# ScalarE's cast of an activation's upper part, issued behind the output copy instead of ahead of it

## The chip, the cores and the metric

The kernel runs on one core of a Trainium2 chip. Its time is the device time in microseconds (us) of one execution; a median over several runs is compared, and less is better. The engines are TensorE (PE; its weight loads are shown as PEld), VectorE (DVE), ScalarE (ACT), GpSimd (POOL) and SyncE (SP, which here only issues DMAs).

## The reference

Agent attention, and behind it a gated feed-forward network over all its outputs:

```python
B, N, C = (4, 12480, 128); n_agents = 49; d_ff = 2048
def sm(a, b):                                  # softmax over the last axis
    s = scale * (a @ b.transpose(0, 2, 1))
    e = np.exp(s - s.max(-1, keepdims=True))
    return e / (e.sum(-1, keepdims=True) + 1e-09)
agent_v = sm(agents, k) @ v
x = (sm(q, agents) @ agent_v).reshape(B * N, C)
h = x @ w_in
out = (h * (1.0 / (1.0 + np.exp(-1.702 * h)))) @ w_out
```

## The kernel before, in words

The work is cut into 52 blocks of 960 tokens (13 for each of the four batches), two halves of 480 columns each. Since agent_v @ w_in is made once per batch (the weights wh and wl), a block's way is: scores of its queries against the 49 agents, softmax, transposed probabilities (q_hi, q_lo), and then 16 slices of 128 of the 2048 hidden columns. The next batch's keys and values are worked off in between, in the first three batches.

Precision is held by splitting 32-bit numbers into an upper and a lower part. Per slice f:

- `up` (L460 on): three pairs of matmuls into two banks `ph`, one for each half of the tokens, and two gelus on ACT (L480), which write `g`.
- `high` (L486 on): `gh`, the upper part of `g`. For even slices, and for 1 and 9, a DMA that POOL issues casts it (L489); for the six others (3, 5, 7, 11, 13, 15) ACT casts it (L491).
- `low` (L494 on): DVE subtracts, `gl` = g - gh (L496).
- `down` (L499 on): three pairs of matmuls, twice per slice, which add the slice's part to the block's output in the two banks `po0` and `po1`.

Most of PE's matmuls use half of its rows, and two run side by side (`half_matmul`, L192); a pair is meant by that. The `po` banks exist once (`ps_o` has one buffer of each), so the next block's first down product can start only when `store` (L522 on) has copied the last block's output out: ACT copies `po0` (L526), DVE copies `po1` (L528), and SP stores both.

No scheduler orders PE, ACT, DVE and POOL: the order in which the code writes their instructions is the order in which they are issued (`manual_schedule`, L847). It is written out gap by gap: `gap(t)` issues first the jobs of that gap (scores, softmax, keys, values), then the up product of a slice with its gelus (`do_up`), the subtraction of the slice three before it (`do_low`), and the down products of the slice six before it (`do_downs`). A block has 17 gaps, k = 0 to 16; in gap 1 there is no up product. In gap 16 `do_downs` holds the block's last down product and then `store`; the slice whose up product and gelus stand in that gap is slice 5 of the next block, one of those that ACT casts. In gap 0 of the next block come its follower's query scores, the up product of slice 6, and the first down product into the `po` banks. A cast by DMA is not issued in its own gap, but at the end of the next one (the list `late`); ACT's cast is written straight behind the gelus:

```python
        if by_dma(f):
            late.append(u)
        else:
            do_high(u)
```

The functions that the change touches, with the line numbers of the profile:

Of the kernel before, what the change touches and what calls it, by code (L numbers as in the profile page):

```python
# [40 lines left out]
def kernel(  # L41
# [140 lines left out]
    def rest():  # L182

        n, ins = order
        if ins is not None and (not rests or rests[-1][0] < n):
            rests.append([n, ins, None])
# [273 lines left out]
    def up(f, wts, pairs):  # L460
        wh, wl = wts
        q_hi, q_lo = pairs
        cols = slice(f * P, (f + 1) * P)
        ph = [ps_h.tile([P, 512], F32, name="ph") for _ in range(2)]
        products = [(wh, q_hi), (wh, q_lo), (wl, q_hi)]
        for k, (w, q) in enumerate(products):
            for c in range(2):
                r = slice(c * H, c * H + A)
                half_matmul(
                    ph[c].name,  # L470
                    c,
                    out=ph[c][:, :CH],
                    lhsT=w[r, cols],
                    rhs=q[r],
                    start=(k == 0),
                    stop=(k == 2),
                )
        g = gpool.tile([P, 2, CH], F32, name="g", bufs=G_BUFS)
        for c in range(2):
            nc.scalar.activation(out=g[:, c, :], in_=ph[c][:, :CH], func=AF.Gelu_apprx_sigmoid)  # L480
        return g

    def by_dma(f):
        return f % 2 == 0 or f in BY_DMA

    def high(f, g):  # L486
        gh = gpool.tile([P, 2, CH], F32R, name="gh", bufs=GH_BUFS)
        if by_dma(f):
            nc.gpsimd.dma_start(out=gh, in_=g)  # L489
        else:  # L490
            nc.scalar.copy(out=gh, in_=g)  # L491
        return gh
# [285 lines left out]
    po = {}  # L778

    late = []  # L780

    def do_high(u):
        gh[u] = high(u % NF, g[u])

    def do_up(u):
        n, f = divmod(u, NF)
        g[u] = up(f, wts[n // NG], pairs[n])
        if by_dma(f):
            late.append(u)
        else:  # L790
            do_high(u)
        if f == NF - 1:
            pairs.pop(n)

    def do_low(u):
        if 0 <= u < steps:
            gl[u] = low(g.pop(u), gh[u])
# [11 lines left out]
    def gap(t):  # L809
        n, k = divmod(t - LAG, GAPS)  # L810
        final = n == B * NG - 1
        if t < LAG:
            u = t
        elif final:
            u = n * NF + LAG + k
        elif k == 1:
            u = None
        else:
            u = n * NF + LAG + max(k - 1, 0)
        before, late[:] = list(late), []  # L820
        rest()
        for job in at.pop(t, ()):
            job()
        if u is not None:
            if u < steps:
                do_up(u)
                rest()
            do_low(u - 3)
        if t >= LAG:
            do_downs(n, k)  # L830
        for u in before:
            do_high(u)

    def do_downs(n, k):
        if k == 0:
            po[n] = [ps_o.tile([P, 512], F32, name=f"po{c}") for c in range(2)]
        first_whole = NF - LAG - 1 if n == B * NG - 1 else NF
        if 0 < k <= first_whole:
            do_down(n, k - 1, True)
        if k < first_whole:  # L840
            do_down(n, k, False)
        elif k < NF:
            do_down_whole(n, k)
        else:
            store(*divmod(n, NG), po.pop(n))

    with tc.manual_schedule(engines={E.PE, E.Activation, E.DVE, E.Pool}):  # L847
        for t in range(gaps):
            gap(t)
# [39 lines left out]
```

## Time and profile before

| | us |
|---|---|
| median of 3 runs (2022.54 to 2028.25) | 2024.57 |
| the profiled execution | 2026.61 |
| its span, first to last instruction | 2024.8 |
| PE busy (share of the span) | 1953.1 (96%) |
| DVE busy | 1553.4 (77%) |
| ACT busy | 1404.0 (69%) |
| POOL busy | 303.4 (15%) |

The profiled execution is one of its own, 2.04 us above the median. Busy time is the union of an engine's instructions. The ends of matmuls are modelled, and a pair's records overlap those of the next, so PE's idle time is a rough figure, and the starts of its matmuls are the sharper one. In a timeline each row gives start and duration in us, engine, line, operation, what it writes and reads, the shape, how many instructions were merged, and in brackets the engine's idle time ahead of it with what ended it.

### The profile page before, as it was taken

What the parts mean: (1) busy time and instruction counts of PE and PEld (TensorE: products, weight loads), DVE (VectorE), ACT (ScalarE), POOL (GpSimd) and SP (SyncE); (2) the same over time, 40 slices, a digit from 0 to 9 for tenths busy, and PEclk for the clock granted to TensorE, in tenths of its full rate; (3) what the DMA queues carried; (4) which work ended last, traced back from release to release, by engine and by line L of the source; (5) the groups of instructions that cost most, each with busy time, mean ns of one, the idle gap of its engine ahead of it and who ended that gap; (6) DMA issues with size and microseconds to landing.
All of it is one profiled execution on the core that took longest, in us unless ns stands there. A gap on an engine that the chain in (4) does not pass through costs nothing.

```text
span 2024.8 us, 59521 instructions
## 1 busy us (share of the span) xinstructions
PE 1953.1 (96%) x25158; PEld 1771.6 (87%) x25158; DVE 1553.4 (77%) x2025; ACT 1404.0 (69%) x2407; POOL 303.4 (15%) x642
## 2 busy tenths in 40 slices
PE   8789999999999999999999999999999999999998
PEld 8578998988988989998988889888898998999987
DVE  5687878887878888887867887888886766676765
ACT  3267777767667667677667677777776787777775
POOL 3011111111111111111111111111111111111111
PEclk9689999999999999999999999999999999999999
DMA  9555565666545665656554566566654544545453
GB/s 256 153 166 178 195 186 183 192 192 195 175 160 191 194 191 184 196 181 182 186 167 167 190 203 190 183 186 186 186 172 139 176 170 172 174 171 180 167 177 137
DMA packets 124336, 365.98 MB, mean 181 GB/s; under 512 B 12572, under 2 KB 38492, under 8 KB 124068
## 3 DMA queue, kind: packets, MB, share of 16 engines
q0 software_dynamic: 74880, 255.62, 36.6%
q1 hardware_dynamic: 49188, 106.55, 19.5%
q8 instruction: 197, 3.23, 0.7%
q14 instruction: 71, 0.58, 0.1%
HBM read 80.97 MB, written 25.56 MB: 53 GB/s over the span
## 4 chain that ended last, share of the span: by engine, by line
PE 80%; ACT 8%; DVE 4%; issue 4%; DMA 3%; SPq 0%; POOL 0%; ACTq 0%; DVEq 0%; POOLq 0%
PE po L192 46%; PE ph L192 24%; PE ps_m L192 7%; ACT g L480 3%; DMA gh<-g 2%; ACT L480 1%; DVE gl L496 1%; ACT L406 1%; PE ph L261 1%; ACT o L526 1%; PE ps_m L383 1%; ACT score L321 1%; DVE rest L173 0%; PE po L657 0%; PE po L518 0%
## 5 line engine op out<-in xcount | busy, mean ns | idle before, releaser
L480 ACT ACTIVATE g<-ph 128x480 f32<-128x480 f32 x1664 | 850.8, 570 | 474.3 <-PE ph L192 469.4
L496 DVE TENSOR_TENSOR gl<-g,gh 128x960 fp32r<-128x960 f32 x832 | 944.5, 1152 | 239.8 <-DMA gh<-g 177.8
L192 PE MATMUL po<-gh,wo_h 64*128 64x480 f32 x3300 | 799.0, 383 | 23.1 <-ACT o L526 18.1
L192 PE MATMUL po<-gl,wo_h 64*128 64x480 f32 x3300 | 789.0, 378 | 0.0
L192 PE MATMUL po<-gh,wo_l 64*128 64x480 f32 x3300 | 787.3, 377 | 0.0
L489 POOL DMA_DIRECT2D gh<-g x520 | 275.2, 529 | 1677.6 <-PE ph L192 799.5
L192 PEld LDWEIGHTS po<-gh,wo_h 64*128 64x128 f32 x3300 | 460.2, 185 | 62.7 <-ACT o L526 36.7
L192 PEld LDWEIGHTS po<-gh,wo_l 64*128 64x128 f32 x3300 | 461.9, 185 | 19.7
L192 PEld LDWEIGHTS po<-gl,wo_h 64*128 64x128 f32 x3300 | 463.2, 186 | 17.0
L192 PE MATMUL ph<-q_hi,wh 49*128 49x480 f32 x1664 | 431.8, 406 | 9.1 <-ACT g L480 8.3
L192 PE MATMUL ph<-q_lo,wh 49*128 49x480 f32 x1664 | 405.6, 380 | 0.0
L192 PE MATMUL ph<-q_hi,wl 49*128 49x480 f32 x1664 | 402.1, 379 | 0.0
L491 ACT CAST gh<-g 128x960 fp32r<-128x960 f32 x312 | 311.5, 998 | 9.9
L192 PEld LDWEIGHTS ph<-q_hi,wh 49*128 49x128 f32 x1664 | 237.5, 186 | 44.6 <-ACT g L480 29.1
L192 PEld LDWEIGHTS ph<-q_hi,wl 49*128 49x128 f32 x1664 | 237.6, 186 | 9.9 <-DVE wl L387 0.2
L192 PEld LDWEIGHTS ph<-q_lo,wh 49*128 49x128 f32 x1664 | 237.3, 188 | 6.1
L192 PE MATMUL ps_m<-ag_part,rest 64*128 64x49 bf16 x4320 | 143.2, 182 | 9.4 <-DVE rest L173 8.3
L192 PEld LDWEIGHTS <-rest 64*128 64x128 bf16 x4320 | 121.9, 94 | 11.9 <-DVE rest L173 11.3
L173 DVE TENSOR_TENSOR rest<-rest 128x488 bf16<-128x488 f32 (+1 forms) x182 | 131.0, 720 | 0.0
L192 PE MATMUL ps_m<-ag_part,qt 64*128 64x49 bf16 x2448 | 85.5, 184 | 0.2 <-DVE acc L354 0.2
L192 PEld LDWEIGHTS <-qt 64*128 64x128 bf16 x2448 | 68.7, 94 | 18.4 <-issue 14.2
L192 PEld LDWEIGHTS <-kt 64*128 64x128 bf16 x1872 | 50.2, 94 | 20.7 <-issue 20.1
(102 smaller groups left out, 1279.7 us busy)
## 6 DMA issues: line engine op xcount, KB each, us to landing
gh<-g POOLq DMA_DIRECT2D x520, 480.0 KB, 3.2
kt<-kT SPq DMA_DIRECT2D x52, 480.0 KB, 4.1
qt<-qT SPq DMA_DIRECT2D x52, 480.0 KB, 4.6
vt<-v SPq DMA_DIRECT2D x52, 480.0 KB, 5.3
outT<-o SPq DMA_DIRECT2D x104, 240.0 KB, 2.4
words<-w_in SPq DMA_DIRECT2D x4, 512.0 KB, 5.9
words<-w_out SPq DMA_DIRECT2D x4, 512.0 KB, 6.4
ag_sb<-agT SPq DMA_DIRECT2D x1, 98.0 KB, 2.0
```

The lines of the kernel that those rows point to most:

```text
L173: nc.vector.tensor_sub(out=halves(r)[1][:, s], in0=r[:, s], in1=halves(r)[0][:, s])
L192: ins = nc.tensor.matmul(tile_position=(c * H, 0), **kw)
L261: nc.tensor.matmul(out=ps[:TB, j * 2 * A : (j + 1) * 2 * A], lhsT=kt[:, c * KB // 2 + j, :], rhs=ag_sb[:, 0:2, :].rearrange("p b a -> p (b ...
L321: nc.scalar.activation(out=sc, in_=sc, func=AF.Exp, scale=scale)
L383: nc.tensor.matmul(out=pw[:, i], lhsT=w["avT"], rhs=w_in_sb[:, s], start=True, stop=True)
L406: nc.scalar.activation(out=e, in_=e, func=AF.Exp, scale=scale)
L480: nc.scalar.activation(out=g[:, c, :], in_=ph[c][:, :CH], func=AF.Gelu_apprx_sigmoid)
L489: nc.gpsimd.dma_start(out=gh, in_=g)
L491: nc.scalar.copy(out=gh, in_=g)
L496: nc.vector.tensor_sub(out=gl, in0=g, in1=gh.bitcast(F32))
L526: nc.scalar.copy(out=o, in_=po[c][:, :CH])
```

## The change

ACT's cast of a slice is no longer issued in `do_up`. The slice is put on a list, `soon`, and its cast is issued at the end of the same gap, behind the down products and, in a block's last gap, behind the output copies; it comes behind the casts by DMA of that gap.

```diff
     late = []
+    soon = []
 ...
         g[u] = up(f, wts[n // NG], pairs[n])
-        if by_dma(f):
-            late.append(u)
-        else:
-            do_high(u)
+        (late if by_dma(f) else soon).append(u)
 ...
         if t >= LAG:
             do_downs(n, k)
-        for u in before:
+        for u in before + soon:
             do_high(u)
+        soon.clear()
```

What this moves: the order of PE's, DVE's and SP's instructions, and what they wait for, is the same in both programs. On ACT, the order differs only around the output copy, once per block. This is ACT at the end of a late block and at the start of the next; `g<-ph` are gelus, two for each slice, `gh<-g` is the cast of one, `o<-po` the copy of the output. Before:

```order
L480 ACTIVATE g<-ph 128x480 x8
L491 CAST gh<-g 128x960
L480 ACTIVATE g<-ph 128x480 x4
L491 CAST gh<-g 128x960
L526 COPY o<-po_34851 128x480
L480 ACTIVATE g<-ph 128x480 x4
L491 CAST gh<-g 128x960
L480 ACTIVATE g<-ph 128x480 x2
L406 ACT_TABLE_LOAD
```

The same place in the changed program:

```order
L480 ACTIVATE g<-ph 128x480 x8
L491 CAST gh<-g 128x960
L480 ACTIVATE g<-ph 128x480 x4
L526 COPY o<-po_34851 128x480
L491 CAST gh<-g 128x960
L480 ACTIVATE g<-ph 128x480 x4
L491 CAST gh<-g 128x960
L480 ACTIVATE g<-ph 128x480 x2
L406 ACT_TABLE_LOAD
```

The copy and the cast of slice 5 have changed places; the other casts, here the one ahead and the one behind, stand where they stood, since no other work of ACT lies between the two places in their gaps. All 51 boundaries between blocks read alike; beside the copy at the run's very end no cast stands.

On POOL, the order is the same, but the tiles `gh` are drawn from their seven buffers in another order, so a casting DMA may wait for other earlier users of its buffer. These are the casts by DMA of slices 1, 2, 4, 6 and 8 around a late boundary, with the semaphores that each waits for. Before:

```order
L489 DMA gh_34113<-g_34064 128x960 [waits PE_49,DMASW5_49,DVE_49,Activation_49]
L489 DMA gh_34144<-g_34095 128x960 [waits PE_49,DVE_49,DMASW6_49,Activation_49]
L489 DMA gh_34202<-g_34155 128x960 [waits PE_49,DVE_49,DMASW7_49,Activation_49]
L489 DMA gh_34336<-g_34261 128x960 [waits PE_49,DVE_49,Activation_49]
L489 DMA gh_34424<-g_34379 128x960 [waits PE_49,DMASW1_49,DVE_49,Activation_49]
```

And in the changed program:

```order
L489 DMA gh_34113<-g_34064 128x960 [waits PE_49,DMASW1_49,DMASW5_49,DVE_49,Activation_49]
L489 DMA gh_34142<-g_34095 128x960 [waits PE_49,DMASW2_49,DVE_49,Activation_49]
L489 DMA gh_34200<-g_34155 128x960 [waits PE_49,DMASW3_49,DVE_49,Activation_49]
L489 DMA gh_34336<-g_34261 128x960 [waits PE_49,DVE_49,Activation_49]
L489 DMA gh_34424<-g_34379 128x960 [waits PE_49,DMASW1_49,DVE_49,Activation_49]
```

[...]

## Rows read from the trace of the kernel before

**Rows 1.** The page, part 1: busy us of each engine, share, instructions

```profile
PE 1953.1 (96%) x25158; PEld 1771.6 (87%) x25158; DVE 1553.4 (77%) x2025; ACT 1404.0 (69%) x2407; POOL 303.4 (15%) x642
```

**Rows 2.** Waits of PE: who waited for whom, us in total, times, longest

```profile
PE po L192 <- ACT o L526: 18.1, 46, 1.1
...
PE po L192 <- DVE o L528: 2.2, 4, 1.3
```

**Rows 3.** Timeline of ACT around one boundary of two blocks

```profile
1820.19 1.03 ACT L480 ACTIVATE g<-ph 128x480 f32<-128x480 f32 x2 [0.94 <-PE ph L192]
1821.26 1.00 ACT L491 CAST gh<-g 128x960 fp32r<-128x960 f32 x1
1822.16 0.55 ACT L526 COPY o<-po 128x480 f32<-128x480 f32 x1
...
1826.40 1.03 ACT L480 ACTIVATE g<-ph 128x480 f32<-128x480 f32 x2 [2.76 <-PE ph L192]
```

**Rows 4.** Timeline of PE at the same boundary

```profile
1821.91 0.45 PE L192 MATMUL ph<-q_hi,wl 49*128 49x480 f32 x2
1822.76 0.49 PE L192 MATMUL po<-gh,wo_h 64*128 64x480 f32 x2 [0.40 <-ACT o L526]
1823.09 0.38 PE L192 MATMUL po<-gl,wo_h 64*128 64x480 f32 x2
...
1823.53 0.25 PE L192 MATMUL ps_m<-ag_part,qt 64*128 64x49 bf16 x6
...
1824.15 0.47 PE L192 MATMUL po<-gh,wo_h 64*128 64x480 f32 x2
```

**Rows 5.** Timeline of DVE at the same boundary

```profile
1821.08 0.67 DVE L528 COPY o<-po 128x480 f32<-128x480 f32 x1
...
1825.44 2.22 DVE L496 TENSOR_TENSOR gl<-g,gh 128x960 fp32r<-128x960 f32 x2
```

**Rows 6.** Timeline of PE inside a block, undisturbed

```profile
1850.40 0.58 PE L192 MATMUL po<-gl,wo_h 64*128 64x480 f32 x2
...
1851.27 0.57 PE L192 MATMUL po<-gh,wo_l 64*128 64x480 f32 x2
```

**Rows 7.** Timeline of PE and DVE at a boundary with DVE's copy later

```profile
715.68 0.64 DVE L528 COPY o<-po 128x480 f32<-128x480 f32 x1
715.77 0.40 PE L192 MATMUL ph<-q_hi,wl 49*128 49x480 f32 x2
...
717.88 0.47 PE L192 MATMUL po<-gh,wo_h 64*128 64x480 f32 x2
```

**Rows 8.** Timeline of PE and DVE at a boundary without a wait for ACT

```profile
1054.92 0.65 DVE L528 COPY o<-po 128x480 f32<-128x480 f32 x1
...
1055.02 0.40 PE L192 MATMUL ph<-q_hi,wl 49*128 49x480 f32 x2
...
1056.93 0.47 PE L192 MATMUL po<-gh,wo_h 64*128 64x480 f32 x1
```

**Rows 9.** Timeline of PE and DVE at a boundary with DVE's copy latest

```profile
1245.42 1.16 DVE L496 TENSOR_TENSOR gl<-g,gh 128x960 fp32r<-128x960 f32 x1 [0.77 <-DMA gh<-g]
...
1245.72 0.39 PE L192 MATMUL ph<-q_hi,wl 49*128 49x480 f32 x2
...
1246.49 0.65 DVE L528 COPY o<-po 128x480 f32<-128x480 f32 x1
...
1247.20 0.48 PE L192 MATMUL po<-gh,wo_h 64*128 64x480 f32 x1 [0.28 <-DVE o L528]
...
1248.51 0.47 PE L192 MATMUL po<-gh,wo_h 64*128 64x480 f32 x1
```

**Rows 10.** Timeline of PE at two other boundaries, the second the run's last

```profile
1283.15 0.49 PE L192 MATMUL po<-gh,wo_h 64*128 64x480 f32 x2 [0.59 <-ACT o L526]
...
1993.42 0.49 PE L192 MATMUL po<-gh,wo_h 64*128 64x480 f32 x2 [1.10 <-ACT o L526]
```

**Rows 11.** The page, part 5: POOL's casting DMAs, busy, mean ns, idle before

```profile
L489 POOL DMA_DIRECT2D gh<-g x520 | 275.2, 529 | 1677.6 <-PE ph L192 799.5
```

## The prediction

> **What bounds the kernel now.** I read the busy shares first: TensorE (PE) is busy for 96% of the span, and ScalarE (ACT), the engine that the change reorders, for 69% [rows 1]. So ACT's order counts only where PE waits for ACT. The waits of PE come next: of all that PE waited for, the largest is ACT's copy of the output, 18.1 us in 46 waits, none over 1.1 us [rows 2]. There are 51 boundaries between two blocks, so this wait stands at 46 of 51, about 0.4 us each.
>
> One boundary shows why. ACT ends the two gelus of the slice at 1821.22, casts until 1822.26, and copies the output only then, 1822.16 to 1822.71 [rows 3]. PE is done with that block's last product long before; it has gone on to the next block's scores and its up product, whose last pair starts at 1821.91, and then needs the bank that ACT has not emptied: the first down product starts at 1822.76, 0.05 us after the copy ended [rows 4]. VectorE (DVE) copies the other half and was done at 1821.75 [rows 5]. So ACT's copy is the last of the two here, and it is late because a cast of about 1 us, which PE needs much later, stands ahead of it.
>
> **What the wait really costs.** The profile's idle time at this boundary is 0.40 us, counted from the end that it gives to the last up matmul. I count from start to start. Undisturbed pairs of 480 columns start every 0.215 us (1850.40 to 1851.27 holds four steps, 0.87 us) [rows 6]. From the first start of the last up pair to the scores behind the first down product there are four such steps, so 0.86 us; it took 1821.91 to 1823.53, 1.62 us [rows 4]. That is 0.76 us lost by the pair's first matmul; its second started 0.07 us later (1821.98), which leaves 0.69 us. I take 0.69, since the later half must be through too. The difference from 0.40 has two parts: a follow-on pair would have started before the modelled end of the one ahead, and the first step after the wait is 0.33 us (1822.76 to 1823.09) instead of 0.215 [rows 4].
>
> [...] By the idle times alone the sum would be the second rival's.
>
> **The change, part by part.** Nothing is added or taken away; PE, DVE and SyncE keep their order. On ACT only one thing per block moves: at the boundary, the copy goes ahead of the cast. At the other five casts of a block no ACT work lies between the old place and the new one, so these cost nothing.
>
> The copy. It can start where the cast stood, 1821.26, and end at 1821.81, about 0.9 us earlier; PE could take the bank 0.05 us later, 1821.86, ahead of the undisturbed start at 1821.91 + 0.215 = 1822.13. DVE's 1821.75 is ahead too. So the wait goes entirely, with 0.27 us to spare. The copy also waits for the down product ahead of it; DVE's copy, which waits for the same product, started at 1821.08, ahead of the gelus' end at 1821.22 [rows 3, 5], so ACT will not stand there. [...]
>
> The cast. It ends where the copy ended before, 0.45 us later than now. Its reader, DVE's subtraction for that slice, is the second of the two that start at 1825.44, so it starts at 1826.50, 3.8 us behind 1822.71 [rows 5]: covered. Past that cover each us would cost 1 us per block.
>
> What is late next in the block? The gelus behind the cast start as now. ACT then stands idle for 2.76 us until the following up product [rows 3], so PE's 0.69 us comes out of that idle time and is not given back; about 2.07 us of it stays.
>
> The buffers of the upper part. They are now taken in another order, so the DMA issues on GpSimd (POOL) wait for other earlier users. These issues mostly wait for PE (799.5 us before their kind) [rows 11], and PE's wait is unchanged in kind; I take 0. What could come of it reaches PE only through DVE's copy, for which PE waited 2.2 us in 4 waits [rows 2], so the bounds are -2.2 and +2.2 us.
>
> The boundaries, read one by one in the timeline, are of five kinds:
> - 29 like the one above, with DVE's copy done in time. At 25 the loss is 0.69 us: 17.3 us. At four PE stands longer; one of them has 0.59 us of idle time where [rows 4] has 0.40 [rows 10], 0.19 us more, so 0.69 + 0.19 = 0.88 us each: 3.5 us.
> - 10 at which DVE's copy ends 0.4 to 0.7 us after the last up pair's start, so DVE takes over. One: from last up pair to second down product 715.77 to 717.88, 2.11 us, DVE's copy ending at 716.32 [rows 7]. A boundary at which ACT was in time and DVE alone was late like that took 1055.02 to 1056.93, 1.91 us [rows 8]. The gain there is 0.20 us; at those where DVE is later it is near none. I take 0.14 on average: 1.4 us.
> - 6 at which DVE's copy is 1 us and more late, as at 1246: PE gets its second half only at 1247.20, released by DVE [rows 9]. Gain 0.
> - 5 without a wait for ACT, such as [rows 8]. Gain 0.
> - The last one, where no scores lie between and PE waits 1.10 us [rows 10]. The copy comes 0.9 us earlier: 0.9 us.
>
> Sum: 17.3 + 3.5 + 1.4 + 0 + 0 + 0.9 = 23.1 us.
>
> **The rivals.**
> First, DVE becomes the later of the two at the 29 good boundaries too. Against it: there its copy mostly ends some 0.2 us ahead of the last up pair's start, and PE's gain shifts both alike. If it happened, each would gain 2.24 - 1.91 = 0.33 us (1821.91 to 1824.15, the second down product [rows 4], against [rows 8]): 9.6 + 1.4 + 0.9 = 11.9 us.
>
> Second, only the idle time of the profile comes back, because the slow restart and the distance to the modelled end have another cause. The idle times at the 29 boundaries add up to 12.2 us, the ten would give 1.1 and the last 0.9: 14.2 us.
>
> Third, slower: the copy, stored 0.9 us earlier, and the loads behind it on SyncE's queue meet the DMAs that cast the even slices, and DVE's subtraction ahead of its copy waits for its cast. [rows 9] has this: 0.77 us of waiting for the DMA, copy done at 1247.14, and PE's second half at 1247.20. There the second down product came 2.79 us after the last up pair (1245.72 to 1248.51), against 2.24 at 1822. If all 29 went so: 29 x 0.55 = 16.0 us slower. It decides from DVE's copy being 0.96 us later than now (1822.71, where ACT's copy ends today, against 1821.75); below that there is a gain. Against it: at 1821 the subtraction ahead of DVE's copy was done by 1821.08, when the copy began [rows 5], before that block's store can be issued, with the change too.
>
> Fourth, the change does nothing that counts: PE waited for something else that becomes ready at the same time. Against it stands the 0.05 us between the copy's end and PE's start at every boundary of the first kind.
>
> **How the numbers follow.** The profiled execution took 2026.61 us (a span of 2024.8), 2.04 us above the median of 2024.57. 2026.61 - 23.1 = 2003.5; against the median 2024.57 - 23.1 = 2001.5, which is the forecast, 1.1% faster. On the same scale the first rival gives 2012.7, the second 2010.4, the third 2040.6, the fourth 2024.6. Chances: forecast 0.73 (with 0.69 to 0.76 per boundary, the buffers' 2.2 us either way and the spread of the runs, 1996.5 to 2007), second rival 0.12, first 0.07, fourth 0.04, third 0.03, and 0.01 for a larger gain. The range reaches from 1996.5 to the second rival with its runs' spread, 2010.8. About 0.3% (6 us) can be told from no change: faster 0.73 + 0.12 + 0.07 + 0.01 = 0.93, same 0.04, slower 0.03.
>
> **What would show it.** In the profile of the changed kernel PE's wait for ACT's copy should fall from 46 waits and 18.1 us to a few, below 2 us; PE's waits for DVE's copy should rise from 4 to some 10 to 20, and 3 to 6 us. The copy should start within 0.1 us of the gelus, the cast right behind it. From last up pair to the scores it should take about 0.87 us where it took 1.62, and ACT's idle time behind the boundary should be near 2.07 us instead of 2.76. Blocks late in the run should be 0.69 us shorter. It would be wrong if PE's waits for DVE's copy took the place of most of the 46, if DVE's waits for the casting DMAs grew, or if PE came to wait for gelus.

## The result, and the profile after

| | before | after |
|---|---|---|
| median, us (range of the runs) | 2025.10 (2022.54 to 2028.25) | 2000.33 (1998.17 to 2000.96) |
| runs | 4 | 4 |
| ratio after / before, 95% interval | | 0.9875 (0.9858 to 0.9892) |
| the profiled execution, us | 2026.61 | 1998.17 |
| its span, us | 2024.8 | 1996.4 |

The changed kernel is 24.8 us faster by the medians; the forecast was 2001.5 us, a gain of 23.1. The two profiled spans differ by more, 28.4 us: the profiled execution of before took 1.5 us more than the median, that of after is the fastest of its runs, and the mean granted clock was 0.986 in the one and 0.988 in the other. So sums below are held against the medians and ratios.

The page of the changed kernel, part 1, answers to [rows 1]:

```profile
PE 1939.8 (97%) x25158; PEld 1811.7 (91%) x25158; DVE 1552.8 (78%) x2025; ACT 1400.7 (70%) x2407; POOL 305.6 (15%) x642
```

Nothing was added or taken away: the instruction counts are the same. ACT's busy share says nothing of the change, since the same work stands in another order.

The waits of PE after, matmuls first, then weight loads (who waited for whom: us in total, times, longest us); they answer to [rows 2]:

```profile
PE ph L192 <- ACT g L480: 8.6, 21, 1.4
...
PE po L192 <- DVE o L528: 7.0, 9, 1.8
...
PEld po L192 <- DVE o L528: 15.3, 21, 2.2
...
PEld po L192 <- ACT o L526: 0.5, 1, 0.5
```

And the same of the weight loads of the kernel before, which stood in no row so far:

```profile
PEld po L192 <- ACT o L526: 36.7, 46, 1.5
...
PEld po L192 <- DVE o L528: 6.1, 11, 1.6
```

The wait for ACT's copy is gone from the matmuls, and one is left among the weight loads. DVE's copy has become the one that PE waits for, at some twenty boundaries.

ACT at the boundary that [rows 3] showed, now at 1797 us (start, duration, instruction, idle time ahead of it and its releaser):

```profile
1796.37 1.04 ACT L480 ACTIVATE g<-ph 128x480 f32<-128x480 f32 x2 [0.92 <-PE ph L192]
1797.29 0.57 ACT L526 COPY o<-po 128x480 f32<-128x480 f32 x1
1797.73 1.02 ACT L491 CAST gh<-g 128x960 fp32r<-128x960 f32 x1
1798.63 1.05 ACT L480 ACTIVATE g<-ph 128x480 f32<-128x480 f32 x2
1801.90 1.04 ACT L480 ACTIVATE g<-ph 128x480 f32<-128x480 f32 x2 [2.21 <-PE ph L192]
```

PE there, as in [rows 4]:

```profile
1798.13 0.45 PE L192 MATMUL ph<-q_hi,wl 49*128 49x480 f32 x2
1798.34 0.46 PE L192 MATMUL po<-gh,wo_h 64*128 64x480 f32 x2
1798.56 0.45 PE L192 MATMUL po<-gl,wo_h 64*128 64x480 f32 x2
1798.78 0.45 PE L192 MATMUL po<-gh,wo_l 64*128 64x480 f32 x2
1799.00 0.27 PE L192 MATMUL ps_m<-ag_part,qt 64*128 64x49 bf16 x4
```

DVE there, as in [rows 5]:

```profile
1797.42 0.65 DVE L528 COPY o<-po 128x480 f32<-128x480 f32 x1
...
1800.97 2.22 DVE L496 TENSOR_TENSOR gl<-g,gh 128x960 fp32r<-128x960 f32 x2
```

The copy starts at 1797.29, 0.12 us ahead of the gelus' end, and the cast right behind it. The first down product follows the last up pair after 0.21 us, where it took 0.85 in [rows 4]; from the last up pair to the scores it takes 0.87 us (1798.13 to 1799.00), not 1.62. Both copies are done before the last up pair starts (1797.86 and 1798.07).

One number for the whole run can be read in the same way at each of 50 boundaries (all but the last, which has no scores): from the start of the second matmul of the last up pair to the next block's second down product, called the **boundary time** below. At this boundary it is 1798.19 to 1799.63, 1.44 us, after 2.17 before (1821.98 to 1824.15 [rows 4]). Its sum is 112.5 us before and 88.3 us after: 24.2 us of the gain lie there.

Up to 2.1 of these 24.2 us need not come from the change. At the boundaries at 186 and 939 us the granted clock of TensorE fell in the profiled execution of before, to a mean of 0.78 over the first (186.65 to 191.26) and 0.55 over the second (939.88 to 942.74); in that of after it was 1.00 over both (185.43 to 189.10 and 928.20 to 929.87). They took 4.61 and 2.86 us before, 3.67 and 1.67 after. For the second of them the rows give the stretch in us, its length, the busy time of each engine and the granted clock, PEclk: before, with PE busy for 2.67 of the 4.20 us ahead of the fall,

```profile
936.00:940.20 4.20, 2.67 (x65) 2.04 (x61) 4.20 (x6) 2.48 (x4) 0.53 (x1) 1.00 0.42 153
940.20:942.90 2.70, 2.70 (x58) 2.14 (x56) 1.28 (x2) 1.03 (x2) 0.21 (x1) 0.50 0.35 126
```

and after, at the same boundary:

```profile
928.50:930.00 1.50, 1.50 (x58) 1.33 (x56) 1.07 (x2) 1.40 (x3) 0.00 (x0) 1.00 0.97 337
```

So a sum of one execution is good to about 1 us for each boundary at which the clock falls (0.94 and 1.19 us here).

### The profile page after: what moved, and what is told of

Same layout as the page of the kernel before. It is cut to its first block, busy times and chain, and to the rows that moved or that the text cites. A ratio compares the mean times of both kernels' runs of the same rounds, so it can differ in the third digit from the quotient of the medians.

```text
span 1996.4 us, 59370 instructions
## 1 busy us (share of the span) xinstructions
PE 1939.8 (97%) x25158; PEld 1811.7 (91%) x25158; DVE 1552.8 (78%) x2025; ACT 1400.7 (70%) x2407; POOL 305.6 (15%) x642
## 4 chain that ended last, share of the span: by engine, by line
PE 85%; ACT 5%; DMA 4%; DVE 4%; issue 2%; SPq 0%; POOL 0%; DVEq 0%; POOLq 0%; ACTq 0%
PE po L192 47%; PE ph L192 26%; PE ps_m L192 8%; DMA gh<-g 3%; ACT g L480 1%; ACT L480 1%; ACT L406 1%; PE ph L261 1%; DVE gl L496 1%; PE ps_m L383 1%; ACT score L321 1%; PE po L657 1%; PE po L518 0%; DVE rest L173 0%; DMA words<-w_in 0%
## 5 line engine op out<-in xcount | busy, mean ns | idle before, releaser
L496 DVE TENSOR_TENSOR gl<-g,gh 128x960 fp32r<-128x960 f32 x832 | 945.6, 1154 | 234.0 <-DMA gh<-g 156.9
L192 PE MATMUL po<-gh,wo_h 64*128 64x480 f32 x3300 | 820.0, 380 | 9.5 <-DVE o L528 7.0
L192 PE MATMUL po<-gl,wo_h 64*128 64x480 f32 x3300 | 812.6, 378 | 0.1
L192 PE MATMUL po<-gh,wo_l 64*128 64x480 f32 x3300 | 809.7, 377 | 0.0
L192 PEld LDWEIGHTS po<-gh,wo_h 64*128 64x128 f32 x3300 | 483.5, 185 | 28.0 <-DVE o L528 15.3
L192 PEld LDWEIGHTS po<-gl,wo_h 64*128 64x128 f32 x3300 | 484.9, 186 | 10.0 <-DVE gl L496 0.5
L192 PEld LDWEIGHTS po<-gh,wo_l 64*128 64x128 f32 x3300 | 483.8, 185 | 10.3
L192 PE MATMUL ph<-q_hi,wh 49*128 49x480 f32 x1664 | 439.0, 405 | 9.3 <-ACT g L480 8.6
L192 PE MATMUL ph<-q_lo,wh 49*128 49x480 f32 x1664 | 412.9, 380 | 0.0
L192 PE MATMUL ph<-q_hi,wl 49*128 49x480 f32 x1664 | 409.7, 378 | 0.0
L192 PEld LDWEIGHTS ph<-q_hi,wh 49*128 49x128 f32 x1664 | 244.6, 186 | 41.0 <-ACT g L480 28.8
```

The source lines that it names most:

```text
L192: ins = nc.tensor.matmul(tile_position=(c * H, 0), **kw)
L496: nc.vector.tensor_sub(out=gl, in0=g, in1=gh.bitcast(F32))
```

## The experiments

Each kernel was run beside the kernel before, whose median differed a little (2023.39 to 2025.10 us), so they are compared by their ratios to it. "ACT's copy" is the copy of `po0`, "DVE's copy" that of `po1`.

### Only one of the six casts moved

```diff
-        (late if by_dma(f) else soon).append(u)
+        if by_dma(f):
+            late.append(u)
+        elif f == LAG - 1:
+            soon.append(u)
+        else:
+            do_high(u)
```

> One part of the change alone: only slice 5's cast, the one beside the output copy, is issued behind the copy; the five other casts of a block are issued straight behind the gelus, so the gh buffers are drawn nearly as before. Theory (the place of the copy on ACT is all): as the changed kernel, about 2000 us, 24 to 25 us below before; PE waits for ACT's copy less than 2 us. Rival (the other order of the gh buffers gives a part): the gain is smaller than the changed kernel's by that part, at most 2.2 us by the bound of the prediction, so 2000 to 2003 us; if the buffers were all, 2025 us.

Measured: 2000.72 us (1996.11 to 2002.93), ratio 0.9878 (0.9861 to 0.9896). That is the changed kernel's 0.9875. The boundary times add up to 89.0 us, 88.3 there; in this execution the granted clock fell at the boundaries at 187 and 933 us (0.80 and 0.67 on average over them). So deferring slice 5's cast gives the whole change in time; the other five are worth nothing that can be measured (each interval reaches some 3.5 us to either side), as the prediction said.

### The casts behind the down products, but ahead of the copies

The diff is against the changed kernel; `highs` issues the casts.

```diff
+        def highs():
+            for u in before + soon:
+                do_high(u)
+            soon.clear()
         if t >= LAG:
-            do_downs(n, k)
-        for u in before + soon:
-            do_high(u)
-        soon.clear()
+            do_downs(n, k, highs)
+        else:
+            highs()
 ...
-    def do_downs(n, k):
+    def do_downs(n, k, highs):
 ...
-        else:
+        highs()
+        if k == NF:
             store(*divmod(n, NG), po.pop(n))
```

> The other part alone: all six casts are issued behind the down products of their gap, with the buffers drawn as in the changed kernel, but ahead of the output copies, so that ACT's order is that of before. Theory: as before, 2025 us within 3 us, with PE waiting for ACT's copy at some 46 boundaries, 18 us. Rival (buffers): below before by the buffers' part, up to 2.2 us; if the buffers were all, 2000 us.

Measured: 2023.65 us (2021.10 to 2026.55), ratio 0.9994 (0.9985 to 1.0003), boundary times 111.5 us (before 112.5). Here the buffers of `gh` are taken in the order of the changed kernel, and ACT keeps the order of the kernel before. PE's wait is back:

```profile
PE po L192 <- ACT o L526: 17.6, 44, 1.1
```

So the order of ACT's copy and cast makes the gain. The order of the buffers, which the prediction had taken as 0 with bounds of 2.2 us, is worth 3 us at the most by the interval's lower end (0.0015 of 2025), about 1 us by its middle, and the interval holds 0.

### More work ahead of ACT's copy, in three sizes

An in-place copy of a weight tile's part on ACT is put ahead of the output copy of the changed kernel. It changes no value, and only delays that copy:

```diff
+                nc.scalar.copy(out=w_in_sb[:, :240], in_=w_in_sb[:, :240])
```

(`:480` and `:960` in the two others.)

> The changed kernel with one more copy on ACT ahead of the output copy, 128x240 in place, estimated 0.3 us from the 128x480 copy's 0.55. In the changed kernel the copy ends 0.3 us ahead of the second start of the last up pair, and PE takes the bank 0.14 us behind that start, so about 0.4 us less the 0.05 us of handing over are free. Count by starts: nearly no cost, 0 to 3 us (five boundaries where the copy ends only 0.13 us ahead pay about 0.2 us each, the last one 0.3), so 2000 to 2003 us. Count by modelled ends (the price of a wait is the idle time that the profile shows): 0 us.

> The same with 128x480, estimated 0.55 us. Count by starts: the copy comes 0.15 us after PE could have started, and a wait costs 0.11 us more for the slow first step, so about 0.25 us at 24 boundaries, 0.45 at five, 0.55 at the last: 9 us (6 to 13) above the changed kernel, 2006 to 2013 us, with hardly any idle time of PE in the profile, since the start still lies ahead of the modelled end. Count by modelled ends: under 1 us above the changed kernel, 2000 to 2002 us.

> The changed kernel with one more copy on ACT ahead of the output copy, 128x960 in place, estimated 1.0 us from the cast of that size: ACT's copy then ends where it ended in the kernel before, though the cast stands behind it. Count by starts: 0.4 to 0.5 us later than with the extra 128x480 (7.1 us above the changed kernel), at nearly all of the 42 boundaries whose weight loads waited for ACT there: 14 to 20 us more, 2021 to 2028 us, the time of before. If something other than the copy's lateness set the time (where the cast stands, or ACT's total work), the time would stay below 2015 us.

The end of ACT's copy and the boundary time are those of the late boundary shown above (the copy's end counted from the last up pair's second start); the sum is that of the 50 boundary times:

| kernel | ACT's copy ends, us | boundary time, us | sum of 50, us | median, us | ratio (interval) |
|---|---|---|---|---|---|
| changed kernel | -0.33 | 1.44 | 88.3 | 2000.33 | 0.9875 (0.9858 to 0.9892) |
| 240 columns | -0.02 | 1.43 | 90.2 | 1997.58 | 0.9869 (0.9849 to 0.9889) |
| 480 columns | +0.18 | 1.62 | 93.4 | 2007.45 | 0.9913 (0.9898 to 0.9927) |
| 960 columns | +0.58 | 2.02 | 106.8 | 2018.52 | 0.9972 (0.9962 to 0.9981) |
| before | +0.72 | 2.17 | 112.5 | 2025.10 | 1 |

With 240 columns the median lies 2.4 us below the expected 2000 to 2003 us, and below that of the changed kernel; the two intervals overlap almost wholly, so what was shown is that this delay costs nothing that can be measured. With 480 columns the time lies in the expected range, with 960 below it, as told further on.

Two things follow. First, at this boundary the price of a late copy rises from nothing, and one for one: a copy that ended 0.18 us behind the last up pair's second start cost 0.18, one at 0.58 cost 0.58, one at 0.72 cost 0.73. A copy that ended before that start was free.

Second, these kernels settle how such a wait is to be counted. With 480 columns PE's waits hardly show it, the weight loads do:

```profile
PE po L192 <- ACT o L527: 0.6, 1, 0.6
...
PEld po L192 <- ACT o L527: 11.4, 42, 1.0
```

```profile
1805.87 0.59 ACT L526 COPY w_in_sb<-w_in_sb 128x480 f32<-128x480 f32 x1
1806.35 0.57 ACT L527 COPY o<-po 128x480 f32<-128x480 f32 x1
...
1806.68 0.45 PE L192 MATMUL ph<-q_hi,wl 49*128 49x480 f32 x2
1806.98 0.49 PE L192 MATMUL po<-gh,wo_h 64*128 64x480 f32 x2
1807.30 0.38 PE L192 MATMUL po<-gl,wo_h 64*128 64x480 f32 x2
```

The second fence is ACT's and PE's timeline of the same kernel (480 columns). The copy ends at 1806.92 and PE's down product starts at 1806.98: it waited. Yet no idle time is printed ahead of it, since the up pair of 1806.68 is drawn until 1807.13. It started 0.30 us behind that pair, not 0.215, and the next step is 0.32 us instead of 0.215: together 0.19 us, which is what the boundary lost. Over the run PE's idle time for ACT's copy is 0.6 us, where the kernel lost 7.7 us against the changed one by the ratios (0.9913 - 0.9875) and 5.1 by the boundary times (93.4 - 88.3).

With 960 columns the expected time was missed, 2.5 us below its lower end. The extra copy lasts as long as the cast, but the whole chain is shorter (ACT and PE of that kernel):

```profile
1815.00 1.03 ACT L480 ACTIVATE g<-ph 128x480 f32<-128x480 f32 x2 [0.93 <-PE ph L192]
1815.91 1.00 ACT L526 COPY w_in_sb<-w_in_sb 128x960 f32<-128x960 f32 x1
1816.80 0.57 ACT L527 COPY o<-po 128x480 f32<-128x480 f32 x1
...
1816.72 0.45 PE L192 MATMUL ph<-q_hi,wl 49*128 49x480 f32 x2
1817.42 0.49 PE L192 MATMUL po<-gh,wo_h 64*128 64x480 f32 x2 [0.25 <-ACT o L527]
```

It starts 0.12 us ahead of the gelus' end (1816.03), while the cast of [rows 3], which reads what the gelus write, starts 0.04 us behind it. So the output copy ends 0.14 us earlier than in the kernel before, and the boundary time is 0.15 us shorter. The sums differ by 5.7 us (112.5 - 106.8), and 5.7 us is what the ratio gives (0.0028 of 2025). The expectation had priced the extra copy as if it were the cast.

### DVE's copy ahead of its subtraction

In the changed kernel DVE's copy is late where the subtraction of the same gap, issued ahead of it, waits for its DMA. In this version the subtraction of gap 16 comes behind the copy:

```diff
-            do_low(u - 3)
+            if k != NF:
+                do_low(u - 3)
         if t >= LAG:
             do_downs(n, k)
+        if u is not None and k == NF:
+            do_low(u - 3)
```

> The changed kernel with the same swap on DVE: at a block's end DVE's copy of the other half is issued ahead of the subtraction of that gap, not behind it. Theory (after the change DVE's copy is the later of the two at some 23 boundaries, where the way from the last up pair to the second down product takes 1.55 to 3.7 us instead of 1.44, 16 us in all): most of these come down to 1.44, 10 to 16 us below the changed kernel, 1985 to 1990 us, and PE's waits for DVE's copy fall from 15 us at the weight loads to below 4. Rival (at those boundaries DVE is behind with other work, and the held subtraction gives back what the copy gains): within 3 us of the changed kernel, with PE waiting for gl or DVE's rest instead.

Measured: 1984.17 us (1979.98 to 1987.25), ratio 0.9801 (0.9786 to 0.9816); boundary times 74.9 us. The median is 0.8 us below the expected 1985 to 1990, and no wait of the weight loads for DVE's copy is left. This is the fastest version of all, by 0.0074 of the time before, some 15 us, faster than the changed kernel. First the changed kernel, PE and then DVE, at the boundary of [rows 9]:

```profile
1229.64 0.39 PE L192 MATMUL ph<-q_hi,wl 49*128 49x480 f32 x2
1229.86 0.38 PE L192 MATMUL po<-gh,wo_h 64*128 64x480 f32 x1
1231.35 0.48 PE L192 MATMUL po<-gh,wo_h 64*128 64x480 f32 x1 [1.11 <-DVE o L528]
...
1229.57 1.16 DVE L496 TENSOR_TENSOR gl<-g,gh 128x960 fp32r<-128x960 f32 x1 [0.99 <-DMA gh<-g]
1230.64 0.65 DVE L528 COPY o<-po 128x480 f32<-128x480 f32 x1
```

And the same boundary of the version with DVE's copy first:

```profile
1220.33 0.39 PE L192 MATMUL ph<-q_hi,wl 49*128 49x480 f32 x2
1220.55 0.39 PE L192 MATMUL po<-gh,wo_h 64*128 64x480 f32 x2
...
1219.17 0.66 DVE L528 COPY o<-po 128x480 f32<-128x480 f32 x1
1219.75 1.15 DVE L496 TENSOR_TENSOR gl<-g,gh 128x960 fp32r<-128x960 f32 x1
```

In the changed kernel the first half's matmul starts on time (1229.86), the second half's only when DVE's copy, held behind a subtraction that waited 0.99 us for its DMA, is done. With the copy first both start together, and the boundary time falls from 3.01 to 1.50 us. What it costs is time of DVE, whose copy now comes early enough to wait for the down product itself:

```profile
DVE o L528 <- PE po L192: 43.7, 30, 2.4
```

That wait was 9.8 us in 20 waits before and 9.6 in 19 in the changed kernel. PE hardly waits for DVE's subtractions in its place: 1.7 us in 3 waits of the weight loads.

### The same swap on DVE alone

The diff is the one above, made to the kernel before, with ACT's order as it was.

> The kernel before with the swap on DVE alone: DVE's copy is issued ahead of the subtraction at a block's end, ACT's order is that of before. Theory (PE waits for the later of the two copies): only boundaries where DVE was later than ACT gain, down to ACT's 2.1 us from the last up pair to the second down product: some 4 us at those with DVE 1 us and more late, some 3 us at the five without a wait for ACT, 8 us in all, 2013 to 2020 us; the two swaps together gained 40 us, more than 25 + 8, since DVE's part is worth 16 only once ACT's copy is early. Rival (the two gains are independent of each other and add up): 16 us, 2009 us or less. Second rival (DVE's swap only counts behind ACT's): 2022 us or more.

Measured: 2017.75 us (2014.34 to 2022.01), ratio 0.9964 (0.9954 to 0.9975); boundary times 104.2 us. PE still waits for ACT:

```profile
PE po L192 <- ACT o L526: 17.3, 44, 1.1
```

In shares of the time before, ACT's swap gives 1.25%, DVE's 0.36%, and both 1.99%. That is more than the sum, because PE needs both banks: at a boundary where both copies are late, either swap alone gains only down to the other copy.

### No cast on ACT for slice 5 at all

The kernel before, with slice 5 cast by a DMA, like slices 1 and 9:

```diff
-BY_DMA = (1, 9)
+BY_DMA = (1, 5, 9)
```

> The kernel before, with slice 5 cast by DMA too: the cast is taken away from ACT at the boundary, so the copy stands straight behind the gelus without any change of order in the gap. Theory (what delayed the copy is the length of the cast ahead of it): about the changed kernel's time, 2000 us, 1997 to 2005. Rival (the gain comes from where the casts are issued, or ACT's copy is not what PE waited for): 2020 us or more. A third way: one more casting DMA per block costs on POOL and in DVE's wait for its landing, 2005 to 2015 us.

Measured: 2003.64 us (1997.23 to 2004.81), ratio 0.9890 (0.9875 to 0.9906); boundary times 90.1 us. Taking the cast away from ahead of the copy gives what moving it behind gave, within the intervals. PE's weight loads wait for DVE's copy as in the changed kernel:

```profile
PEld po L192 <- DVE o L528: 14.1, 20, 2.2
```

DVE's waits for casting DMAs rise here to 189.3 us in 126 waits (before 177.8 in 126, changed kernel 156.9 in 118), and no gain or loss of time beyond the intervals goes with it.

## Why the prediction was right, and where its terms were off

The mechanism held: the first two experiments give all of the gain to the one place where ACT's copy went ahead of slice 5's cast. The terms, by boundary times of before and after:

| kind of boundary, as the prediction sorted them | forecast gain, us | measured, us |
|---|---|---|
| 25 with DVE's copy in time | 17.3 | 17.3 |
| 4 where PE stood longer | 3.5 | 3.6 |
| 10 with DVE's copy 0.4 to 0.7 us late | 1.4 | 1.7 |
| 6 with DVE's copy 1 us and more late | 0 | 0.4 |
| 5 without a wait for ACT | 0 | 1.2 |
| the last | 0.9 | 1.0 |
| sum | 23.1 | 25.2 |

The last one, which has no scores, is counted from the last up pair to the next up pair. Before, these are lines of PE's timeline around the second of [rows 10]:

```profile
1991.75 0.56 PE L192 MATMUL ph<-q_hi,wl 49*128 49x480 f32 x2
...
1994.18 0.38 PE L192 MATMUL ph<-q_hi,wh 49*128 49x480 f32 x2
```

and after:

```profile
1964.35 0.52 PE L192 MATMUL ph<-q_hi,wl 49*128 49x480 f32 x2
1964.99 0.48 PE L192 MATMUL po<-gh,wo_h 64*128 64x480 f32 x2
...
1965.74 0.38 PE L192 MATMUL ph<-q_hi,wh 49*128 49x480 f32 x2
```

2.43 us became 1.39. The sum of 25.2 is 0.4 us above the 24.8 between the medians, well inside their interval (21.9 to 28.8 us). At two boundaries, one among the 6 and one among the 5, the clock fell before and not after, and they alone hold 0.9 and 1.2 us; the other 49 give 23.1. That this is the forecast's very sum is in part luck, since errors cancelled in it:

**The 0.69 us.** Two errors cancelled in the first row. At 22 of the 25 boundaries the gain was 0.73 us on average: the 0.07 us by which the pair's second matmul starts later should not have been taken off, because in the undisturbed case it starts later as well (1798.13 and 1798.19 after). At the three others, 0.42, 0.30 and 0.56 us were gained, because DVE's copy, in time there before, ended 0.28 to 0.55 us after the last up pair's start with the change. That is the first rival, at three boundaries instead of 29. That nothing is given back later shows in the late blocks: from the boundary at 1753.72 to that at 1958.54 six blocks took 204.82 us before, and 200.39 after (1731.40 to 1931.79), 0.74 us less for each. The forecast was 0.69.

**Counting by starts.** The second rival, that only the profile's idle time comes back, is refuted by the kernel with 480 columns above: 0.6 us idle there, 5 to 8 us lost. There the wait is hidden under an up pair that is drawn 0.15 us past the next start (1807.13 against 1806.98). The pairs inside a block speak for the count by starts too: a pair there is drawn for 0.57 us, and the next starts 0.215 us after its start [rows 6].

**DVE as the next one late.** Right in kind, too small in size. Expected were 10 to 20 waits of 3 to 6 us in all. The matmuls show 9 waits and 7.0 us, the weight loads 21 and 15.3. By boundary times 23 boundaries are above 1.52 us, and exceed 1.44 us by 16.4 us together. Taking DVE's lateness away gave back 13.4 of these (88.3 - 74.9), and about 15 us of the time. The prediction judged the matmuls' waits alone, the row that it had just shown to count too little. At the 16 boundaries where DVE's copy was late before too, the time moved by 0.23 us for the worse to 0.72 for the better (0.93 at the one where the clock fell before), as DVE's copy came earlier or later than there, and the forecasts of 0.14 and 0 us for each hold only for their sums.

**The cast and ACT's idle time.** The cast's reader, the second subtraction of the 1800.97 row, starts half of 2.22 us later, at about 1802, and the cast ended at 1798.75: covered. ACT's idle time behind the boundary is 2.21 us where 2.07 was forecast. The missing part is the hand-over: the copy starts 0.12 us ahead of the gelus' end, where the cast started 0.04 behind it, so ACT's chain of copy, cast and gelus is shorter. From the boundary's gelus' end to that of the next gelus it took 2.42 us before (1821.22 to 1823.64 [rows 3]), and 2.27 after (1797.41 to 1799.68).

**The other rivals.** The third, that earlier stores and late DMAs make it slower, did not happen: DVE's waits for casting DMAs fell from 177.8 to 156.9 us. The fourth is refuted by the ratio. ACT never waited at the head of its queue for a down product of the boundary: its only wait for one is the run's last copy (7.8 us before and after), so no run shows what a waiting copy would have held up there.

## What to carry to other kernels

Where an engine empties the only copy of an accumulator's bank, nothing that is needed later should stand ahead of that in its queue (here a cast of 1.00 us did, and moving it gave 1.25%); where two engines empty the two halves, look at both queues at once: here the later one decided, and the second swap was worth twice as much after the first (0.74% against 0.36%). Price a wait of TensorE from start to start against an undisturbed stretch, and look at the waits of the weight loads too: with 480 columns the idle time of the matmuls showed 0.6 us, that of the weight loads 11.4, and the kernel lost 5 to 8. The price here was only what ended after the next needed start: a delay that ended 0.02 us before it, with 240 columns, was free (0.9869 against 0.9875).

## What the runs showed of the hardware that was not expected

**Starts on ACT differed with what the instruction reads.** At all 51 boundaries of the changed kernel the copy, which reads another tile, started 0.11 to 0.12 us ahead of the end of the gelus before it; at all 312 casts of the kernel before the cast, which reads the gelus' own output, started 0.03 us behind it. Moved behind the copy, the same cast starts 0.13 us ahead of its end (1797.73 against 1797.86), and the copy behind the cast started, before, 0.10 us ahead of the cast's end (1822.16 against 1822.26 [rows 3]). So these starts overlap by 0.10 to 0.13 us where the next one doesn't read the last one's output, and not at all where it does.

**A wait of TensorE came with a longer first step.** At 39 boundaries of the kernel before both halves of PE start together behind ACT's copy, and at all of them the first step is 0.32 to 0.33 us instead of 0.215. It is 0.32 in the kernel with 480 columns too, where PE started only 0.09 us late.

**Two small delays came with the new order.** ACT's copy took 551 ns before and 568 after (medians). That it now runs beside DVE's copy is not the reason: with 960 columns put ahead, DVE's copy is over before ACT's begins, and ACT's takes 572 ns. It took 551 ns wherever the cast stands right ahead of it (the kernel before, the casts ahead of the copies, DVE's swap alone) and 567 to 572 where gelus or the extra copy do. What follows it makes no difference: with slice 5 cast by a DMA gelus follow it, as before, and it takes 567. Why, no run shows. The output stores landed after 2.4 us in the kernel before and after 3.0 in the changed one, 2.6 with 480 columns and 2.4 with 960. In these four the two copies end 0.99, 0.28, 0.46 and 0.85 us apart (medians): the closer, the longer. But it was 2.9 us at 0.05 us apart with DVE's copy first, and 3.9 at 0.23 with slice 5 cast by a DMA, so the distance alone doesn't set it, and what does is open. PE waits for neither delay.
